# Moving the second norm of half the tokens into the MLP's first half, with five steps of the second matmul summed in DRAM

## The chip, the cores and the metric

The kernel runs on one core of one Trainium2 chip. The metric is the device time of one launch in microseconds. A core has a matrix engine (TensorE, PE in the profile), a vector engine (VectorE, DVE), a scalar engine (ScalarE, ACT), a general engine (GpSimd, POOL) and a queue processor (SyncE, SP). SP and POOL also issue the transfers, on a queue each, in program order. Operands live in SBUF, 128 partitions wide; TensorE writes to PSUM, eight banks of 128 x 512 fp32, and VectorE or ScalarE have to carry the results out. DRAM is the memory beyond.

## What is computed

An adaLN block on 2048 tokens of width 1024: a norm with a scale and a shift from a condition, a Fourier mixing over tokens and width, a gated residual, a second norm with scale and shift, an MLP with 3584 hidden columns, and a second gated residual.

```python
mod = (silu(c) @ w_mod).reshape(1, 6, 1, 1024)
sa, ca, ga, sb, cb, gb = (mod[:, n] for n in range(6))
h = layernorm(x) * (1 + ca) + sa
a, b = h @ dft_hid_re.T, h @ dft_hid_im.T
x = x + ga * (dft_seq_re @ a - dft_seq_im @ b)
h = layernorm(x) * (1 + cb) + sb
x = x + gb * (gelu(h @ w1 + b1) @ w2 + b2)
```

All inputs and the output are fp32.

## The kernel before

Every large product runs in fp16 with each fp32 operand split into a high and a low half, three passes a product. The split takes a copy on ScalarE (the high half) and a subtraction on VectorE (the low half).

**The head** is the part up to the MLP: the first norm, the Fourier transform along the width with its symmetries folded, then the transform along the tokens (`seq_pair`, L3057) in eight blocks b of 256 tokens. For each block `seq_pair` issues two groups of matmuls, Q and P, and two evictions (L3102, L3107). `ln2` (L3171) multiplies by ga (L3213), adds x with an accumulating transfer into SBUF ("xa"), stores the residual stream to the output ("x1", L3225 on SP and L2171 on POOL), and runs the second norm: squares on ScalarE (L3187), subtraction and scale (L3235), a root with one Newton step on 128 x 2 numbers (L2630 to L2639), scale and shift (L3239), squares again, a root again, and a last pass on ScalarE (L3248). `z_psum` (L3347) transposes the block on TensorE (L3368), forms the differences that a seven-product scheme needs with more matmuls (L3376), and splits them from PSUM into fp16 (L3389 on ScalarE, L3416 on VectorE). Block 7 takes `turn` (L3251) and `z_tasks` (L3271), which form the differences on VectorE. The operands of blocks 0 to 3, the first token half, stay in SBUF at `O_ZC`. Those of blocks 4 to 7 go to DRAM (`zc_d`, "fzc" in the profile) on POOL's queue, and `reload` brings them back at chunk 13.

**The MLP** has 28 chunks g of 256 hidden columns: 0 to 13 for the first token half, 14 to 27 for the second. `gemm3(g)` (matmuls at L3843) makes the 256 hidden columns for 1024 tokens with seven products of 12 matmuls, in the order 0, 1, 2, 4, 3, 6, 5. Products share three PSUM banks "a", "g" and "b", from which ScalarE (L3865, gelu at L3862) and VectorE (L3869) evict. Chunks 0 and 1 are made by `gemm3_first` (gelu at L4156). `gemm4(v)` (L3957) multiplies two chunks by their rows of w2, with 14 products in two blocks `blk`. After each product the running sum `acc` (32 KB a partition, at `O_ACC` = 48) is updated: at v = 0 and 7, the first step of each half, four of seven products are copied on ScalarE (L3997) and three added on VectorE (L4007); at all others VectorE does all seven. The chunks run as 0, 1, 2, v = 0, then 3, 4, v = 1, and so on.

During v = 0 to 6, VectorE and ScalarE also split the weights from fp32 to fp16 (L2398, L2410, L2424), after a norm of each piece that sets its scale (L3497, a reduction on POOL at L3509), and SP stores the fp16 pieces (`w1_d`, `w2_d`, "fw"). The second half loads them from there. `w1c` holds two chunks, 14 slots. The bias rows gb x b2 are added to the output by 16 accumulating transfers (`gbb_rows`, L4203, issue at L4208) during chunks 3 to 8.

**The order of the work** is written by a planner in the file that runs when the kernel is built. A task has an engine, a cost, dependencies and a due time; `pick` takes, of the tasks that could start, those due first, and `need` and `emitted` force what a step depends on. Costs are estimates: a root counts 0.4 us on ScalarE, a product `PE12` = 12 x 0.2165 us. Engines then run their lists in order and wait on semaphores.

In the head the planner works on a clock in which the MLP's tasks have due times behind the blocks':

```python
due = 110.0 + 22.0 * b if b < NB - 1 else 300.0
f = lambda: act.activation(dst, src, AF.Gelu_apprx_tanh, scale=inv, bias=b1s[:, 2 * p + j : 2 * p + j + 1])
add("gelu", "act", 0.8, f, [*deps, ("root", NB - 1)], ("quad", g, n), 266.0)
```

The last line makes every gelu wait for the last root of the last block.

Of the kernel before, what the change touches and what calls it, by code (L numbers as in the profile page):

```python
# [9 lines left out]
F32 = mybir.dt.float32  # L10
# [1981 lines left out]
def fast(ctx, tc, x, cre, cim, dre, dim, w1, b1, w2, b2, c, wm, out):  # L1992
# [69 lines left out]
    YW, ZT0 = [((8832, 10880), (12928, 14976), (0, 2048))[b % 3] for b in range(8)], 17024  # L2062
    YW[5] = (53248, 2048)
# [6 lines left out]
    def junk2(key):  # L2070
        return at({("s1", 0): 149.375, ("s1", 1): 46104 / 256, ("s1", 2): 46104 / 256}.get(key, 28.375), 1024, F16).rearrange("p (s x) -> p s x", s=2)
# [32 lines left out]
    def zt(n):  # L2104
        return FA(ZT0 + 1024 * n, (1, 1024))

# [10 lines left out]
    w1c = at(0, 14336, F16).rearrange("p (m s a x) -> p m s a x", m=7, s=2, a=2)  # L2117
# [13 lines left out]
    def raw2(v, q):  # L2131
        return at(O_K + 4 * q, 1024).rearrange("p (s x) -> p s x", s=2)
# [7 lines left out]
    row_d = {n: dram.tile([P, D], F32, tag=f"frow_{n}", name=f"frow_{n}") for n in ("gbb", "gb")}  # L2140
# [61 lines left out]
    class Task:  # L2202
# [16 lines left out]
        def run(self):  # L2219
# [8 lines left out]
            if not in_order[0] and self.eng in ("dma", "st"):  # L2228

                b = self.cost if self.eng == "dma" else 0.8  # L2230
# [38 lines left out]

    def pick_first(until):  # L2270

        first, best = {}, {}
        for q in sorted((q for q in streams.values() if q), key=lambda q: q[0].due):
            t = q[0]
            st = t.start()
            if st > until or st > 1e11:
                continue
# [12 lines left out]
    def pick(until):  # L2290
# [6 lines left out]
        for q in sorted((q for q in streams.values() if q), key=lambda q: q[0].due):  # L2297
# [6 lines left out]
            if t.eng == "dma":  # L2304
# [4 lines left out]
                continue  # L2309
            if best is not None and best[2] or st + t.cost > until:  # L2310
                continue
# [13 lines left out]
    def fill_to(until):  # L2325
        while True:
# [3 lines left out]
            q.popleft().run()  # L2330

# [53 lines left out]
    def split_tasks(q, outs, scale, n, src, res, after, post, last_use, free=None):  # L2385
# [9 lines left out]
        def hi(m, j):  # L2395
# [4 lines left out]
            was = [last_use(k) for k in tup(m)] if last_use is not None else []  # L2400
            t = Task("act", 0.17 + 0.87 * n * len(tup(m)) / 1024, f, reads(j) + was + [free(m) if free else None])
# [483 lines left out]
    def row(n, j):  # L2885
# [57 lines left out]
        add("rowa", "act", 1.1, last_, [k, "mod"], ("rowe", n), due)  # L2943
        if n == 3:
# [112 lines left out]
    def seq_pair(b):  # L3057
# [54 lines left out]
        if b == 5:  # L3112
            deps += [("P", 3), ("Q", 3)]
# [40 lines left out]
    ADDED = (0, 7)  # L3154
# [16 lines left out]
    def ln2(b):  # L3171
        y, w, cl = yb(b), wb(b), lns[b % 3]
# [28 lines left out]
        wfree = w_free(b)  # L3201
        h, k_ = divmod(b, 4)
        yr = FA(YW[b][0] + 1024, (-1, 1024))
        for n in (1, 0):
# [16 lines left out]
            x1[n] = k  # L3221
            if n:
# [5 lines left out]
        else:  # L3228
            step("dve", 0.17, lambda: dve.scalar_tensor_tensor(
                nm, su, -1.0 / D, cm[:, h, k_], op0=ALU.mult, op1=ALU.subtract), ["cm"])  # L3230
# [20 lines left out]
    def turn(i):  # L3251
        b, n = divmod(i, 2)
        ps = PA(6 * 512, (1, 1024))
        due = 100.0 + 11.0 * i

        def f():
            for d in range(ND):
                pe.transpose(ps[:, d * P : (d + 1) * P], wb(b)[:, n, d * P : (d + 1) * P], ident[:, :])

        add("seqt", "pe", 1.5, f, [("w", i), *([("zt", i - 1)] if n else zlast[6] + zlast[7])], ("turn", i), due)  # L3260

        def ev():
            if n and b > 3:
                v = zt(n).rearrange("p (d t) -> p d t", t=P)
                act.activation(v, PA(6 * 512 + P - 1, (P, ND), (-1, P)), AF.Copy)
            else:
                act.activation(zt(n), ps, AF.Copy)

        add("zte", "act", 1.1, ev, [("turn", i)], ("zt", i), due)

    def z_tasks(b):  # L3271
        h, k = divmod(b, 4)
        made = []
        stage = 512 * 184 + 256 if b < NB - 1 else 512 * O_K

        def q(i, j=None):

            o = [ZT0 + 1024 * (n % 2) + 512 * (n // 2) for n in (i, i if j is None else j)]
            return FA(o[0], (o[1] - o[0], 2), (1, 512)) if j is not None else FA(o[0], (1, 512))

        def places(ms, a):
            if h == 0:
                o = [512 * O_ZC[m] + 2048 * a + 512 * k for m in ms]
            else:
                o = [stage + 1024 * made.index(m) + 512 * a for m in ms]
            return HA(o[0], (o[1] - o[0], 2), (1, 512)) if len(ms) > 1 else HA(o[0], (1, 512))

        def hi(ms, js, deps):
            def f():
                if h:  # L3290
                    for m in ms:
                        if 4 < b < NB - 1:
                            reuse("z", (b - 1, len(made)))
                        made.append(m)
                act.activation(places(ms, 0), q(*js), AF.Copy)

            n0 = order.index(ms[0])
            free = [slot("z", (b - 1, n0 + i)) for i in range(len(ms))] if 4 < b < NB - 1 else []
            add("z", "act", 0.17 + 0.44 * len(ms), f, deps + free, (b, "zhi", ms), due, f"z{b}")
            return (b, "zhi", ms)  # L3300

        def lo(ms, js, deps):
            def f():
                dve.tensor_tensor(places(ms, 1), q(*js), places(ms, 0), op=ALU.subtract)  # L3304
                for m in ms:
                    if h:
                        n = made.index(m)
                        dst = zc_d[m][:, :, k].rearrange("p a c t -> p a (c t)")
                        v = HA(stage + 1024 * n, (512, 2), (1, 512))
                        store("z", (b, n), lambda dst=dst, v=v: gp.dma_start(dst, v), ("z", b, m), tag=f"z{b}")  # L3310
                    done["z", b, m] = done[t]

            t = add("z", "dve", 0.13 + 0.54 * len(ms), f, deps, (b, "zlo", ms), due, f"z{b}")
            return t

        def comb(d, a, c, deps, key):
# [991 lines left out]
```

## Time and profile before

| what | value |
|---|---|
| median of 3 runs | 1344.61 us |
| lowest and highest | 1339.23 and 1344.76 us |
| the profiled execution | 1344.03 us |
| its span | 1342.2 us |
| mean granted TensorE clock | 0.962 |
| busy share PE, DVE, ACT, POOL | 92%, 79%, 54%, 19% |
| moved by transfers | 285.23 MB, 213 GB/s |

The profile is one execution. Its busy share of PE counts pipelined matmuls, so a full row of nines says that TensorE always had a matmul under way. The slices and the stretches of time tell where it had not. Waits are given with the engine and line that released them. A line of the code can stand for many shapes and stages: L4007 is one line for all steps of the second matmul, and L2398, L2410 and L2424 are helpers that every split of weights and hidden values goes through.

### The profile page before, as it was taken

Reading aid. Unit: us, or ns where it says so; the run is one execution under the profiler, and the core shown is the slowest. Engines: PE = TensorE matmul, PEld = TensorE weight load, DVE = VectorE, ACT = ScalarE, POOL = GpSimd, SP = SyncE. Lnnn points to the kernel's source line nnn. Section 1 sums busy time; section 2 is a strip of 40 time slices with the busy share of each in tenths; the row PEclk is TensorE's granted clock in tenths of the full one; section 3 lists DMA queues with packets and bytes.
Section 4 is the critical chain, followed back from the end, with each engine's and each line's share of the span. In section 5 each row is a group of like instructions: output and inputs, shape, how many; then the busy total and the mean of one; then the engine's idle time right before and its main releaser. Section 6 shows DMA issues by size and latency. Waiting matters only on the chain.

```text
span 1342.2 us, 16824 instructions
## 1 busy us (share of the span) xinstructions
PE 1230.5 (92%) x5923; PEld 579.8 (43%) x5923; DVE 1060.8 (79%) x1601; ACT 731.1 (54%) x1186; POOL 249.8 (19%) x381
## 2 busy tenths in 40 slices
PE   3568886868999999999999999999999999999997
PEld 0225444544444444444444444444444444444443
DVE  5798777885888898989899896566777868586785
ACT  4785546777767566574746351466455553526330
POOL 2000022332011101010000001435243242233101
PEclk9779787879999999999999999999999999999999
DMA  9966366887269767583625386968595766585155
GB/s 364 389 214 218 117 228 173 188 280 269 97 221 263 227 196 224 162 238 114 220 93 191 118 336 174 287 221 302 199 325 182 234 230 196 190 295 177 56 177 116
DMA packets 103686, 285.23 MB, mean 213 GB/s; under 512 B 13116, under 2 KB 13132, under 8 KB 101672
## 3 DMA queue, kind: packets, MB, share of 16 engines
q1 hardware_dynamic: 75160, 191.44, 41.0%
q0 software_dynamic: 28432, 92.63, 24.2%
q8 instruction: 48, 0.79, 0.2%
q14 instruction: 46, 0.38, 0.1%
HBM read 199.08 MB, written 84.93 MB: 212 GB/s over the span
## 4 chain that ended last, share of the span: by engine, by line
PE 66%; DVE 4%; ACT 2%; DMA 2%; issue 1%; POOL 0%; SPq 0%; DVEq 0%; ACTq 0%; POOLq 0%
PE ps L3957 34%; PE ps L3843 32%; DVE arena L2410 2%; DMA arena<-in_w_dram 1%; ACT arena L2398 1%; DVE arena L2424 1%; DVE arena L4007 1%; DMA fzc<-arena 1%; DVE arena L3869 0%; ACT ps L3497 0%; ACT arena L3862 0%; DVE arena L4059 0%; DVE arena L3304 0%; ACT arena L4156 0%; ACT arena L3997 0%
## 5 line engine op out<-in xcount | busy, mean ns | idle before, releaser
L3843 PE MATMUL ps<-arena 128*128 128x512 f16 x2352 | 513.6, 380 | 5.5 <-ACT arena L3865 3.5
L3957 PE MATMUL ps<-arena 128*128 128x512 f16 x2352 | 510.9, 379 | 2.7 <-DVE arena L4007 1.6
L3843 PEld LDWEIGHTS <-arena 128*128 128x128 f16 x2352 | 230.4, 98 | 285.2 <-issue 7.6
L3957 PEld LDWEIGHTS <-arena 128*128 128x128 f16 x2352 | 230.0, 98 | 281.3 <-issue 3.7
L4007 DVE SCALAR_TENSOR_TENSOR arena<-ps,i4c,arena 128x1024 f32<-128x1024 f32 x179 | 229.3, 1281 | 94.2 <-PE ps L3957 90.0
L2398 ACT ACTIVATE arena<-arena,shc 128x512 f16<-128x512 f32 (+1 forms) x115 | 116.2, 1017 | 129.9 <-DVE arena L2424 74.4
L3727 ACT ACTIVATE arena<-arena 128x512 f32<-128x512 f32 (+4 forms) x159 | 97.2, 613 | 108.6 <-DVE arena L3736 84.5
L2410 DVE SCALAR_TENSOR_TENSOR arena<-arena,shc 128x512 f16<-128x512 f32 (+1 forms) x115 | 128.8, 1121 | 32.4 <-ACT arena L2398 31.9
L2424 DVE TENSOR_TENSOR arena<-arena 128x512 f32<-128x512 f32 (+1 forms) x196 | 148.8, 764 | 4.0
L3862 ACT ACTIVATE arena<-arena,b1s,i1c 128x512 f32<-128x512 f32 x78 | 63.4, 813 | 89.7 <-DVE arena L3869 86.8
L2398 ACT ACTIVATE arena<-arena,s1c 128x512 f16<-128x512 f32 (+1 forms) x70 | 60.7, 886 | 75.6 <-DVE arena L2424 46.3
L3736 DVE TENSOR_TENSOR arena<-arena 128x256 f32<-128x256 f32 x240 | 87.8, 420 | 1.2 <-DMA arena<-in_cre_dram,idxs 0.7
L3869 DVE TENSOR_TENSOR arena<-arena,ps 128x512 f32<-128x512 f32 x78 | 53.4, 685 | 44.1 <-PE ps L3843 42.6
L3509 POOL PARTITION_ALL_REDUCE sums<-sums x21 | 9.2, 444 | 422.7 <-DVE sums L3505 410.3
L2410 DVE SCALAR_TENSOR_TENSOR arena<-arena,s1c 128x512 f16<-128x512 f32 (+1 forms) x70 | 65.8, 958 | 7.2 <-ACT arena L2398 6.9
L3865 ACT ACTIVATE arena<-ps 128x512 f32<-128x512 f32 x78 | 46.0, 589 | 36.1 <-PE ps L3843 36.0
L2410 DVE SCALAR_TENSOR_TENSOR arena<-arena,s2c 128x1024 f16<-128x1024 f32 x49 | 61.9, 1279 | 4.4 <-ACT arena L2398 4.4
L3497 ACT ACTIVATE ps<-arena 128x1024 f32<-128x1024 f32 x46 | 46.7, 1014 | 17.8 <-DMA arena<-in_w_dram 12.2
L2398 ACT ACTIVATE arena<-arena,s2c 128x1024 f16<-128x1024 f32 x49 | 55.0, 1137 | 1.5 <-DVE arena L2424 1.5
L3017 PE MATMUL ps<-arena 128*128 128x256 f16 (+5 forms) x297 | 43.9, 296 | 6.5 <-ACT arena L2796 3.2
L3187 ACT ACTIVATE arena<-arena,lns 128x1024 f32<-128x1024 f32 x32 | 36.6, 1144 | 21.9 <-DMA arena<-in_x_dram,idxm 5.7
L3773 POOL DMA_DIRECT2D arena<-in_cim_dram x69 | 38.1, 558 | 53.1 <-ACT arena L3727 29.0
(239 smaller groups left out, 1123.7 us busy)
## 6 DMA issues: line engine op xcount, KB each, us to landing
fw<-arena SPq DMA_DIRECT2D x71, 512.0 KB
arena<-fw SPq DMA_DIRECT2D x119, 256.0 KB
arena<-fw SPq DMA_DIRECT2D x49, 512.0 KB
arena<-in_wm_dram SPq DMA_DIRECT2D x32, 512.0 KB
arena<-in_w_dram SPq DMA_DIRECT2D x32, 512.0 KB
arena<-in_cre_dram POOLq DMA_DIRECT2D x64, 256.0 KB
arena<-in_cim_dram POOLq DMA_DIRECT2D x64, 256.0 KB
arena<-in_w_dram SPq DMA_DIRECT2D x56, 256.0 KB
```

The costliest lines, as they stand in the source:

```text
L2398: act.activation(o[m][0], q(j), AF.Copy, **sc)
L2410: dve.scalar_tensor_tensor(o[m][1], q(j), scale, o[m][0], op0=ALU.mult, op1=ALU.subtract)
L2424: dve.tensor_tensor(q(d), q(a), q(b), op=op)
L3497: act.activation(junk, parts[j][0], AF.Square, accum_out=t[:, j : j + 1])
L3727: f = lambda: act.activation(v, v, AF.Square, accum_out=csum[0:pn, n : n + 1])
L3736: return lambda: dve.tensor_tensor(dst[0][:, o::2], src[0][:, o::2], dst[0][:, o::2], op=op)
L3843: pe.matmul(ps.rearrange("p (k t) -> p k t", k=4), w1c[:, m, s, a, d * P : (d + 1) * P], zc(m)[:, b, :, d, :], start=(start and d == 0 and ...
L3862: act.activation(dst, src, AF.Gelu_apprx_tanh, scale=inv, bias=b1s[:, 2 * p + j : 2 * p + j + 1])
L3865: after_pe("act", 0.5, lambda: act.activation(quad(g)[:, n], ps[b], AF.Copy), kp[b])
L3869: after_pe("dve", 0.6, lambda: dve.tensor_tensor(q, q, ps[b], op=ALU.add), kp[b])
L3957: pe.matmul(t[:, j], hidc[:, c_, m, a, k * P : (k + 1) * P], w2c[:, m, c_, w], start=(start and c_ == 0 and n == 0), stop=(c_ == 1 and n = ...
L4007: lambda: dve.scalar_tensor_tensor(dst, ps[b], inv, dst, op0=ALU.mult, op1=ALU.add), kp[b],
```

## The change

Blocks 4 to 7 are called HELD. In the head they keep only `seq_pair`, the product with ga, the residual and its store, and the mean. Everything from the squares to the fp16 operands moves to a new function, `z_held`, which works in place on one block at a time, as one chain of steps: blocks 4 and 5 (EARLY_LN = 2) from the copy in SBUF, planned around the MLP's first chunks; blocks 6 and 7 from a copy that is stored to DRAM (`x1_d`) and loaded again, due 100 and 200 us after chunk 2. The rows cb and sb are stored to DRAM; sb is loaded again for every held block, cb for 6 and 7.

```diff
+    HELD = (4, 5, 6, 7)
+    EARLY_LN, W1N = 2, 10
+    def w1_slot(g, m):
+        return (7 * g + ORDER.index(m)) % W1N
...
+            if b in HELD[EARLY_LN:]:
+                store("x1s", i, lambda n=n: sp.dma_start(x1_d[b][:, n], y[:, n]), k)
...
+        if held_:
+            return
...
-        if b < NB - 1:
+        if b not in HELD:
             z_psum(b)
-        else:
-            for n in range(2):
-                turn(2 * b + n)
-            z_tasks(b)
```

`z_held` holds the same passes as `ln2`, with two groups of eight transposes and the differences on VectorE:

```diff
+    def z_held(b, v):
...
+        for n in range(2):
+            step("act", 1.35, sq(n, 1.0, nm), [ld[n], ("nm", b), *(turned(1) if early else [])])
...
+        for n in range(2):
+            step("dve", 1.28, under(n), [k_cb, *([("st", "x1", 2 * b + n)] if early else [])], ("u", b, n))
+        soon.clear()
+        k_sb = load_row("sb", [("st", "crow", 2), *([("P", 7), ("Q", 7)] if v else [])] if early else [])
+        root(0.25 / D, eps4)
...
+        root(0.25 / (SZ * SZ * D**3), epsz)
...
+        for n in range(2):
+            step("pe", 1.1, turn(n), [] if n or not early else zlast[6] if not v else [("held_t", HELD[0])])
+            step("act", 1.1, ev(n), [], ("held_t", b) if n else None)
...
+        hi((0, 1), (0, 2))
+        lo((0, 1), (0, 2))
+        comb((0, 1), (1, 1), (0, 3))
...
+    def due_at(v):
+        return due[3, 2] + 100.0 * (v - 1) if v >= EARLY_LN else 262.0 + 8 * v
```

The gelus of chunks 0 and 1 wait for the last root of block 3 in place of block 7. Chunk 0 uses PSUM banks 3 to 5 in place of 0 to 2. The second block of `gemm4(0)` needs block 4 to be finished, since its running sum lies where block 4 is worked on.

In the second matmul, steps v = 0 to 4 each start `acc` anew (four of seven products copied on ScalarE, three added on VectorE), and their result goes to DRAM; from v = 1 on the transfer adds to what is there. Before v = 5 the sum is loaded back.

```diff
+    def dump(v, blk, m, r, hf, src):
+        dst = acc_d[:, blk, :, r, 512 * hf : 512 * hf + 512]
+        op = {"accum_op": ALU.add} if v else {}
+        store("dump", (v, blk, m), lambda: gp.dma_start(dst, src, **op), ("acc", blk, m), tag=f"dump{v}")
+        if v == NDUMP - 1:
+            f = lambda: sp.dma_start(src, dst)
+            push("back", "back", [Task("dma", 1.5, f, [("st", "dump", (v, blk, m))], ("back", blk, r, hf))], due[4, v + 1] - 30.0)
...
-        first, end = u == 0, v == NPAIR - 1
+        first, end = u == 0 or v < NDUMP, v == NPAIR - 1
...
+        if 0 < v <= NDUMP:
+            need(f"dump{v - 1}", "back")
```

The fp16 pieces of w1 stand in a ring of 10 slots in place of 14, which frees 8 KB a partition. The first piece of w2 is loaded once, earlier and to another place, in place of twice; the next piece's loads no longer wait for block 7. A product calls `turns()`, which puts transposes that are ready ahead of it. The bias rows move from chunks 3 to 8 to chunks 12 and 13:

```diff
     def gbb_rows():
         need("n2_0")
-        t = at(28, 1024)
+        need(*(f"z{b}" for b in HELD))
+        t = at(20, 1024)
...
-            g, m = divmod(i * 42 // NS, 7)
-            push("gbb", "gbb", [Task("pool", 1.5, f, [("g3", 3 + g, ORDER[m])])], 1e6)
+            g, m = divmod(i * 14 // NS, 7)
+            push("gbb", "gbb", [Task("pool", 1.5, f, [("g3", 12 + g, ORDER[m])])], 1e6)
...
-            if g == 2:
+            if g == 11:
                 gbb_rows()
```

More of the change, by code (lines that the diff above doesn't have):

```diff
@@ L4200, in fast @@
     later[0] = True
+    for v, b in enumerate(HELD):
+        if v >= EARLY_LN:
+            z_held(b, v)
     load_w1(3, 0, 1)
```

332 lines of the change are left out of this document (190 added, 142 removed).

## The prediction

> **What bounds the kernel now.** I read the page's slices first, then TensorE in order of time, then its waits, then busy time by stage.
>
> ```profile
> span 1342.2 us, 16824 instructions
> ...
> PE   3568886868999999999999999999999999999997
> ...
> DVE  5798777885888898989899896566777868586785
> ACT  4785546777767566574746351466455553526330
> PEclk9779787879999999999999999999999999999999
> ```
>
> One slice is 33.6 us. PE is full from the tenth slice to the end, and has holes before it, where DVE is busy and the granted clock is lower. So there are two regimes, and the border is what the change can move. TensorE around it, in order of time (columns: start, duration, what, count, idle time before it):
>
> ```profile
> 262.07 2.66 PE L3368 MATMUL ps<-ident,arena 128*128 128x128 f32 x20 [0.58 <-ACT arena L3248]
> ...
> 283.52 2.75 PE L3843 MATMUL ps<-arena 128*128 128x512 f16 x12
> ...
> 304.10 4.45 PE L3843 MATMUL ps<-arena 128*128 128x512 f16 x12 [2.01 <-DMA arena<-fw]
> ...
> 334.91 31.24 PE L3843 MATMUL ps<-arena 128*128 128x512 f16 x144
> 365.99 5.34 PE L3957 MATMUL ps<-arena 128*128 128x512 f16 x24
> ```
>
> L3843 is the first MLP matmul; its first product (12 matmuls) comes at 283.5. By 334.9 only 9 of 21 are done, because the pieces of second norms 4 to 7 lie between them. From there it runs without a break: 144 matmuls, 12 products, take 31.1 us to 365.99, so **2.59 us a product**. At 365.99 the second matmul (L3957) begins, and the remaining 976.2 us of the span (1342.2 - 366.0) are almost pure matmul, as the waits say, before 345 us in the first two rows and after it in the others:
>
> ```profile
> PE ps L3368 <- ACT arena L3248: 17.4, 4, 8.4
> PE ps L3376 <- DVE arena L3416: 8.1, 5, 3.3
> ...
> PE ps L3843 <- ACT arena L3865: 3.5, 3, 2.0
> PE ps L3957 <- DVE arena L4007: 1.6, 3, 1.2
> PE ps L3957 <- ACT arena L3997: 0.8, 2, 0.4
> ```
>
> The head waits for the norm's last pass (L3248) and the fp16 split (L3416), which run on ScalarE and VectorE. By stage (columns of each engine: busy us; then clock, DMA share, GB/s):
>
> ```profile
> 200.00:260.00 60.00, 42.02 (x227) 29.19 (x226) 48.39 (x92) 39.71 (x66) 16.46 (x13) 0.80 0.74 190
> 260.00:335.00 75.00, 57.97 (x294) 32.60 (x292) 56.76 (x111) 58.78 (x92) 23.12 (x28) 0.88 0.82 261
> ...
> 366.00:439.00 73.00, 68.78 (x316) 30.73 (x315) 62.84 (x98) 52.80 (x69) 11.85 (x17) 1.00 0.79 241
> 439.00:511.00 72.00, 71.85 (x334) 32.55 (x333) 67.04 (x94) 43.11 (x57) 5.57 (x8) 1.00 0.72 205
> 511.00:584.00 73.00, 73.00 (x340) 33.04 (x338) 66.89 (x96) 43.62 (x58) 5.55 (x8) 1.00 0.68 199
> 584.00:657.00 73.00, 73.00 (x340) 33.09 (x338) 65.65 (x93) 41.75 (x55) 1.15 (x3) 1.00 0.49 172
> ```
>
> PE idles 35 us between 200 and 335; with three blocks' transposes (2.66 us a block by the row at 262) and their correction matmuls this bounds what can be won at about 45 us. The last four rows are the steps v = 0 to 3: there VectorE is about 90% busy, ScalarE only 57 to 72%.
>
> **Part 1: norms 4 to 7 leave the head.** The MLP's first half needs blocks 0 to 3 only. Its third product needs block 3's last split; VectorE in that stretch:
>
> ```profile
> 264.32 2.48 DVE L3235 SCALAR_TENSOR_TENSOR arena<-arena,lns 128x1024 f32<-128x1024 f32 x2 [0.34 <-ACT arena L3187]
> ...
> 268.70 1.28 DVE L3239 SCALAR_TENSOR_TENSOR arena<-arena,lns 128x1024 f32<-128x1024 f32 x1
> ...
> 273.85 0.16 DVE L2637 TENSOR_TENSOR lns<-lns 128x2 f32<-128x2 f32 x1
> ...
> 280.44 1.23 DVE L3416 TENSOR_TENSOR arena<-ps,arena 128x1024 f16<-128x1024 f32 x1 [1.06 <-ACT arena L3389]
> ```
>
> Pairs of L3235 and L3239 come once a block, so these are block 4's: 2.48 + 2 x 1.28 + nine small ones of 0.16 = 6.5 us that leave the queue ahead of block 3's last split, which ended at 281.7. So it ends at about 275. The y evictions of blocks 4 to 7 stay (bound: if all of those of 5 and 6 slip behind it, 268). Two products are possible before it; the other 19 take 49.2 us: second matmul at 324. On the way lie transfers. SyncE's queue is in order, and today stands behind stores that wait for x to land:
>
> ```profile
> SPq L3225 <- DMA arena<-in_x_dram: 58.6, 6, 21.0
> ```
>
> The w1 loads of the first chunks stand in that queue, now with the second copies of blocks 6 and 7 and two row loads, without the second load of w2. Bounds: 0 and one such wait of 21 us; I take 4, since the stream's own worst wait so far was 2.0. **Second matmul at 328 instead of 366.** If blocks 4 and 5 are not hidden beside these 21 products, this fails first.
>
> **Part 2: what the MLP's first half takes on.** Rows by shape:
>
> ```profile
> L3187 ACT ACTIVATE arena<-arena,lns 128x1024 f32<-128x1024 f32 x30 | 34.3, 1144 | 16.2 <-DMA arena<-in_x_dram,idxm 5.7 <-issue 5.3 <-DMA arena<-in_x_dram 3.0
> L3187 ACT ACTIVATION_READ_ACCUMULATOR arena<-arena,lns 128x1 f32 x30 | 5.7, 188 | 0.0
> L3248 ACT ACTIVATE arena<-arena,lns 128x1024 f32<-128x1024 f32 x16 | 19.1, 1234 | 6.9 <-DVE lns L3246 6.9
> L3258 PE MATMUL ps<-ident,arena 128*128 128x128 f32 x16 | 2.1, 276 | 0.4 <-ACT arena L3267 0.4
> L4156 ACT ACT_TABLE_LOAD x1 | 1.3, 1283 | 0.0
> ...
> L3997 ACT ACTIVATE arena<-ps,i4c x16: 1093/1114/1116, 370.6 to 915.6; 128x1024 f32<-128x1024 f32 x16
> ...
> L4007 DVE SCALAR_TENSOR_TENSOR arena<-ps,i4c,arena 128x1024 f32<-128x1024 f32 x179 | 229.3, 1281 | 94.2 <-PE ps L3957 90.0
> ```
>
> PE: two times 8 transposes a block, 2.1 us; block 4's lie beside the head, three blocks cost **6.3 us**.
> VectorE: 8 evictions a step go over to ScalarE for v = 1 to 4, 32 x 1.28 = 41 us off. A held block adds 2.5 + 2.6 + 1.4 as above, the splits 3 x 1.23 + 0.7 and some 2.6 of differences: 13.5; three add 40.5. Even, still over 90%.
> ScalarE: 8 x 1.11 = 8.9 us more a step; a block adds four squares with their reads (5.3), two passes of L3248 (2.4), and about 7 of copies and roots: 14.6.
>
> **The rule that speaks against it.** In this trace the only table load of the MLP stands before the first gelu, because all roots are done by then. After the change the eight roots of four blocks fall among gelus: up to 16 loads of 1.28 = 20.5 us. With four a block (5.1) ScalarE does 181.3 (the four steps) + 3 x 8.9 + 3 x 19.7 = 267 of 291 us, 92%. The Trainium skill, "ScalarE: Activation LUTs", section "Table sets: the hidden batching unit", says to batch calls by set; its "What ACT_TABLE_LOAD costs" gives 1283 ns, which the row has, and a drain of about 1380 ns more, which no run here shows (the gelu follows at once); 16 such switches would be an estimated 42.6 us.
>
> How much of it reaches PE: two products on one bank pair have another between them, 2.59 us, so an eviction of 1.11 can be 1.5 late; one table load fits, two do not. Bounds: 0, and all 20.5. I take **6 us** for the pressure on both engines, half a microsecond for each of the 12 late loads; the four steps had some 4 until now.
>
> ```profile
> L4208 POOL DMA_DIRECT2D out_dram<-arena x16: 854/1158/1577, 409.5 to 573.7; - x16
> ```
>
> Sums in DRAM: 40 stores of 512 KB on POOL's queue, each read back or added to a step later, about 36 us of first matmuls away; nothing on PE waits nearer. They replace 16 accumulates of bias rows there, and v = 3 has a DMA share of 0.49. I cost them at nothing; uncovered, one landing of some 5 us a step.
>
> Ring of w1 slots, 14 to 10: a slot is refilled 9 products ahead, 23 us; nothing, while VectorE keeps up.
>
> Those 16 bias rows now meet the reload of the second half's operands:
>
> ```profile
> 775.00:780.00 5.00, 5.00 (x25) 2.25 (x23) 4.89 (x6) 1.41 (x2) 0.00 (x0) 1.00 0.98 398
> ...
> 795.00:800.00 5.00, 5.00 (x25) 2.27 (x24) 4.47 (x6) 3.84 (x5) 0.00 (x0) 1.00 1.04 403
> ...
> 773.15 8.09 SPq L3437 DMA_DIRECT2D arena<-fzc  x4
> ```
>
> The DMA engines are full there, at 400 GB/s, and half of the rows (4 MB) would take 10 us of it, between 0 and 10 on PE: I take **4**, since the next chunk needs the operands one by one over 18 us.
>
> **Sum:** 328 + 976.2 + 6.3 + 6 + 4 = 1320.5 of span; around it lay 1.8 (1344.03 - 1342.2): **1322 us**. The median shown is 0.6 above that execution, which I leave out. Its own range is 1301 (268 for block 3, no stalls) to 1336.
>
> **Rivals.**
> A. The head becomes bound by transfers: DMA share is 0.82 already, and one 21 us wait sits before the w1 loads. Second matmul at 345: 1339. Against: 7 MB leave the head (21 stores of 256 KB to fzc, four loads of 512 KB), 4 enter.
> B. Slower: **ScalarE becomes the bound** in v = 1 to 4, its evictions late at every product. From 0.25 us a product over 112 products (28 us) on, the gain is gone; at 0.5 us it is 56 instead of 6: 1372. For: 92% on both engines, bound to each other in order. Against: 16 evictions on ScalarE (L3997) made PE wait 0.8 in all, with ScalarE at 72%.
> C. Table switches, each in front of an eviction: 20.5 in place of 6: 1337. By the Trainium skill's drain as well (page and section above) it would be an estimated 1359.
> D. It doesn't do what it says: blocks 4 and 5 stay ahead of the second matmul on VectorE, 2 x 13.5 us of the 38 gained, and splits of w2 wait behind them: 1322 + 27 = 1349, no change.
>
> **Chances.** Forecast 0.60, A 0.10, B 0.15, C 0.08, D 0.07. A measurement of this kernel can tell about 0.5% (6.7 us) from no change: faster ends at 1337.9. Forecast, half of A and half of C are faster: 0.69; the rest of A and C and D the same: 0.16; B slower: 0.15. The range runs from 1301 to 1349, so that D is within and B, with a few hundredths below, is left out.
>
> **What would show it.** Second matmul (the line of L3957) first at 322 to 335; block 3's last split at 270 to 278; no L3248 of blocks 4 to 7 ahead of the first product. Table loads: up to 16, after the first gelu. PE's waits for ScalarE after 345 us under 15 in all; if far more, B or C. A wait for fzc near the reload of 2 to 8. Wrong it is if PE starts early and then pays it back in holes in v = 0 to 4.

## The result and the profile after

The kernel became slower: 1473.38 us median of 4 runs (1468.47 to 1476.79) against 1343.09 us for the kernel before on the same chip. The ratio is 1.0972 with a 95% interval of 1.0929 to 1.1015, so 130 us were lost where 22 were forecast to be won. No rival of the prediction had a time near this; the slowest, B, had 1372. Two versions further down had one run each far longer than its others (2775.13 and 2154.89 us), and their medians are of the other three. The profiled execution took 1468.47 us. First its page: the span, then the slices of PE, DVE and ACT and the granted clock (a line of three dots stands for rows left out).

```profile
span 1466.7 us, 16907 instructions
...
PE   3567976948989669886989687899999999999996
...
DVE  5788778826777476784947586556676777677784
ACT  4875557628867557673756233236644454536330
...
PEclk9788887979999879998998988999999999999999
```

One slice is 36.7 us. PE has holes up to the 26th slice, some 950 us, where before it was full from the tenth on; behind that it is full as it was. In four of its deepest slices from there (the 9th, 14th, 19th and 23rd) VectorE is at 2, 4, 4 and 5 tenths and ScalarE at 2, 5, 3 and 2. There the engines wait, they do not work. TensorE in order of time, at the head's end:

```profile
274.74 2.75 PE L3915 MATMUL ps<-arena 128*128 128x512 f16 x12
277.82 23.47 PE L3915 MATMUL ps<-arena 128*128 128x512 f16 x108 [0.32 <-DVE arena L3498]
311.74 8.15 PE L3915 MATMUL ps<-arena 128*128 128x512 f16 x24 [10.45 <-DMA arena<-fw]
329.20 10.54 PE L3915 MATMUL ps<-arena 128*128 128x512 f16 x36 [9.31 <-ACT arena L4245]
...
362.35 1.89 PE L4042 MATMUL ps<-arena 128*128 128x512 f16 x8
```

L3915 is the first MLP matmul (L3843 before), L4042 the second (L3957 before). The head starts as forecast: the second product waits 0.32 us for block 3's split (L3498) and starts at 277.82, and ten products are done by 301.3. Then come 10.45 us for weights and 9.31 for an eviction, and the second matmul begins at **362.35**, not at 328. SP's queue, VectorE's next instruction and ScalarE's tell why (start, duration, and in brackets idle time and what ended it):

```profile
285.06 17.09 SPq L3262 DMA_DIRECT2D out_dram<-arena  x2
...
306.04 3.51 SPq L3746 DMA_DIRECT2D arena<-fw  x4
...
317.14 0.47 SPq L3330 DMA_DIRECT2D arena<-frow_sb  x1
```

```profile
324.85 1.28 DVE L3354 SCALAR_TENSOR_TENSOR arena<-arena,csum 128x1024 f32<-128x1024 f32 x1 [25.36 <-DMA arena<-frow_sb]
```

```profile
327.43 1.15 ACT L3318 ACTIVATE arena<-arena,csum 128x1024 f16<-128x1024 f32 x1 [25.51 <-DVE arena L3354]
...
328.58 0.57 ACT L4245 ACTIVATE arena<-ps 128x512 f32<-128x512 f32 x1
```

SP stands for 17 us at the residual stores of the held blocks (L3262), which wait for x to land. Behind them in its one queue are the weights of the first chunks (L3746) and the load of the row sb for block 4 (L3330), issued only at 317.14. VectorE's next instruction (L3354, block 4's scale and shift) waits 25.36 us for that row, ScalarE's squares of the block (L3318) wait 25.51 us for VectorE, and behind them in ScalarE's list stands the eviction (L4245) that TensorE waited 9.31 us for.

Then the steps v = 0 to 3, in the stretches of before (busy us of PE, PEld, DVE, ACT, POOL, then clock, DMA share, GB/s; the sum of all four in the last row):

```profile
...
511.00:584.00 73.00, 57.24 (x243) 24.72 (x243) 50.55 (x70) 45.77 (x61) 12.78 (x17) 0.85 0.69 209
...
sum 291.00, PE 243.06 PEld 109.14 DVE 209.46 ACT 200.42 POOL 53.62; mean PE 60.76 PEld 27.28 DVE 52.37 ACT 50.10 POOL 13.40
```

PE is busy 243 of 291 us. VectorE sank from 90% to 72% (209.5 of 291), ScalarE is at 69% (200.4 of 291), though ScalarE was given more to do in a step and VectorE, by the prediction's sum, as much as before. The granted clock falls to 0.85 in the stretch with most holes, and a matmul takes 0.236 us there on the average (57.24 us for 243) where it took 0.215 before (73.00 for 340). PE's waits from 345 to 950 us (us in total, times, longest):

```profile
PE ps L3915 <- ACT arena L3937: 33.5, 7, 21.6
PE ps L4042 <- ACT arena L4081: 29.3, 7, 12.1
PE ps L4042 <- DVE arena L4092: 25.2, 3, 16.3
PE ps L3915 <- DMA arena<-fzc: 9.7, 3, 3.9
```

All but the last are evictions, but an eviction as such takes about a microsecond, so a wait of 21.6 us is the end of a longer chain. One such chain, from PE back through ScalarE and VectorE to POOL:

```profile
523.34 6.86 PE L3915 MATMUL ps<-arena 128*128 128x512 f16 x18 [21.55 <-ACT arena L3937]
```

```profile
520.96 0.81 ACT L3934 ACTIVATE arena<-arena,b1s,i1c 128x512 f32<-128x512 f32 x1 [22.93 <-DVE arena L3941]
```

```profile
518.28 0.15 DVE L3591 TENSOR_SCALAR sums<-sums 128x1 f32<-128x1 f32 x1 [23.16 <-POOL sums L3587]
```

```profile
498.03 1.21 POOL L4002 DMA_DIRECT2D facc<-arena  x1 [7.19 <-issue]
504.80 1.21 POOL L4002 DMA_DIRECT2D facc<-arena  x1 [5.57 <-issue]
510.92 1.21 POOL L4002 DMA_DIRECT2D facc<-arena  x1 [4.90 <-issue]
...
517.15 0.73 POOL L3417 DMA_DIRECT2D fzc<-arena  x1 [4.26 <-issue]
517.77 0.47 POOL L3587 PARTITION_ALL_REDUCE sums<-sums  x1
```

L4002 is the store of the sums. An accumulating one takes 1.22 us on POOL, but the next mostly starts only 6 to 8 us after the one before (9.6 at most in a row of them), in 11 cases with nothing in the profile that it waits for ("issue"). VectorE is idle from 495 to 518, so it isn't VectorE's work that holds the stores up. Behind three of them and two stores to fzc stands the reduction of a weight piece's norm (L3587, L3509 before), 0.47 us long. VectorE (L3591) needs its result to scale the next split, and stands from 495 to 518. Behind that stands VectorE's eviction L3941; ScalarE's gelu (L3934) waits 22.93 us for it, and the eviction L3937 that TensorE needs stands behind the gelu. VectorE's wait for that reduction, 345 to 950 us in the kernel after and from 366 in the kernel before:

```profile
DVE sums L3591 <- POOL sums L3587: 88.1, 12, 23.2
```

```profile
DVE sums L3513 <- POOL sums L3509: 5.3, 9, 0.6
```

### The profile page after: what moved, and what is told of

It is laid out like the page before. It is cut to its first block, busy times and chain, and to the rows that moved or that the text cites. A ratio compares the mean times of both kernels' runs of the same rounds, so it can differ in the third digit from the quotient of the medians.

```text
span 1466.7 us, 16907 instructions
## 1 busy us (share of the span) xinstructions
PE 1250.3 (85%) x5881; PEld 579.8 (40%) x5881; DVE 1029.4 (70%) x1576; ACT 784.6 (53%) x1236; POOL 300.6 (20%) x430
## 3 DMA queue, kind: packets, MB, share of 16 engines
q0 software_dynamic: 39584, 118.32, 31.1%
## 4 chain that ended last, share of the span: by engine, by line
PE 55%; DVE 14%; issue 11%; DMA 10%; ACT 7%; POOL 2%; SPq 0%; DVEq 0%; POOLq 0%; ACTq 0%
PE ps L4042 26%; PE ps L3915 25%; DVE arena L2433 3%; ACT arena L2420 2%; DMA arena<-in_wm_dram 2%; DMA arena<-fzc 2%; DMA arena<-in_x_dram 2%; DVE arena L2447 1%; DMA arena<-in_x_dram,idxm 1%; PE ps L3043 1%; DVE arena L4092 1%; POOL facc L4002 1%; DMA arena<-in_w_dram 1%; DVE arena L3498 1%; DVE arena L3278 1%
## 5 line engine op out<-in xcount | busy, mean ns | idle before, releaser
L3915 PE MATMUL ps<-arena 128*128 128x512 f16 x2352 | 528.4, 387 | 66.2 <-ACT arena L3937 33.5
L4042 PE MATMUL ps<-arena 128*128 128x512 f16 x2352 | 526.4, 386 | 57.0 <-ACT arena L4081 29.3
L3915 PEld LDWEIGHTS <-arena 128*128 128x128 f16 x2352 | 233.4, 99 | 357.5 <-issue 77.6
L4042 PEld LDWEIGHTS <-arena 128*128 128x128 f16 x2352 | 233.1, 99 | 346.6 <-issue 74.3
L4092 DVE SCALAR_TENSOR_TENSOR arena<-ps,i4c,arena 128x1024 f32<-128x1024 f32 x147 | 188.4, 1282 | 97.0 <-PE ps L4042 94.8
L3934 ACT ACTIVATE arena<-arena,b1s,i1c 128x512 f32<-128x512 f32 x78 | 63.5, 814 | 122.5 <-DVE arena L3941 122.3
L4002 POOL DMA_DIRECT2D facc<-arena x40 | 44.9, 1124 | 230.4 <-DVE arena L4092 87.5
L3941 DVE TENSOR_TENSOR arena<-arena,ps 128x512 f32<-128x512 f32 x78 | 53.3, 684 | 54.2 <-PE ps L3915 52.2
L3937 ACT ACTIVATE arena<-ps 128x512 f32<-128x512 f32 x78 | 46.0, 589 | 43.6 <-PE ps L3915 42.5
L4081 ACT ACTIVATE arena<-ps,i4c 128x1024 f32<-128x1024 f32 x48 | 52.8, 1104 | 28.0 <-PE ps L4042 25.6
L3591 DVE TENSOR_SCALAR sums<-sums 128x1 f32<-128x1 f32 x21 | 3.2, 151 | 92.0 <-POOL sums L3587 92.0
L3043 PE MATMUL ps<-arena 128*128 128x256 f16 (+5 forms) x297 | 47.1, 309 | 9.3 <-DVE arena L2575 3.4
```

The lines of the kernel that those rows point to most:

```text
L3043: pe.matmul(PA(bp + o, (1, w), pn=m), l, r, start=i == 0, stop=i == len(mm_) - 1)
L3915: pe.matmul(ps.rearrange("p (k t) -> p k t", k=4), w1at(g, m)[:, a, d * P : (d + 1) * P], zc(m)[:, b, :, d, :], start=(start and d == 0 an ...
L3941: after_pe("dve", 0.6, lambda: dve.tensor_tensor(q, q, ps[b], op=ALU.add), kp[b])
L4002: store("dump", (v, blk, m), lambda: gp.dma_start(dst, src, **op), ("acc", blk, m), tag=f"dump{v}")
L4042: pe.matmul(t[:, j], hidc[:, c_, m, a, k * P : (k + 1) * P], w2c[:, m, c_, w], start=(start and c_ == 0 and n == 0), stop=(c_ == 1 and n = ...
L4092: lambda: dve.scalar_tensor_tensor(dst, ps[b], inv, dst, op0=ALU.mult, op1=ALU.add), kp[b],
```

## The experiments

Each was timed against the kernel before on the same chip. Ratios are to that kernel, with 95% intervals; differences between versions are of medians.

**The sums in eight DRAM tensors instead of one.** It asks whether the stores wait for each other because they write to one tensor.

```diff
-    acc_d = dram.tile([P, 2, 2, 2, D], F32, tag="facc", name="facc")
+    acc_d = {k: dram.tile([P, 2, 512], F32, tag=f"facc_{k}", name=f"facc_{k}") for k in range(8)}
...
-        dst = acc_d[:, blk, :, r, 512 * hf : 512 * hf + 512]
+        dst = acc_d[4 * blk + 2 * r + hf][:, :, :]
```

> The changed kernel, but the running sums in DRAM are eight tensors (one for each quadrant of each block) in place of one; plan, queues and bytes are the same. Theory P (POOL's queue): each of the 40 stores to the one tensor waits until the store before it has landed, 6 to 8 us apart, and the norm's sums over partitions stand behind them in POOL's queue. Then VectorE's wait for those sums falls from 88 us to under 25, and the time from 1473 to 1385 to 1415 us. Rival B (ScalarE and VectorE overloaded, the one of the prediction): within 1% of 1473. Rival Q (the transfers as such are too many): within 1% of 1473.

Measured: 1470.97 us, 1.0956 (1.0915 to 1.0998), the same as with one tensor. That the stores form a chain by their tensor (theory P) is refuted. Rivals B and Q both had this time.

**No sums in DRAM.** `acc` stays in SBUF and is added to at every step, all else as in the change.

```diff
-    NDUMP = 5
+    NDUMP = 0
...
```

> The changed kernel without the sums in DRAM: the running sum stays in SBUF as before, VectorE adds at all steps but v = 0 and 7; norms 4 to 7 stay within the MLP's first half. Theory P: as e1_tiles, 1380 to 1415 us, since no store stands in POOL's queue. Rival B: VectorE gets 41 us back, so no faster than the changed kernel, 1470 to 1500. Rival Q: 20 MB of accumulating transfers less, about 1400.

Measured: 1396.46 us, 1.0405 (1.0368 to 1.0443): 77 us of the 130 go with the stores, though VectorE has the 41 us of additions back that they saved it. Rival B, by which this would not be faster, fails here; P's range and Q's (about 1400) both hold the result. The second matmul still came first at 363.46. VectorE's wait for the reduction is as good as gone:

```profile
DVE sums L3591 <- POOL sums L3587: 8.8, 8, 3.0
```

**The stores alone, in the kernel before.** 32 extra stores of the running sum in v = 1 to 4, of the same shape and on POOL, from v = 2 on accumulating; nothing reads them. Once into one tensor, once into eight.

```diff
...
+    def dump(v, blk, m, r, hf, src):
+        dst = acc_d[:, blk, :, r, 512 * hf : 512 * hf + 512]
+        op = {"accum_op": ALU.add} if v > 1 else {}
+        store("dump", (v, blk, m), lambda: gp.dma_start(dst, src, **op), ("acc", blk, m), tag=f"dump{v}")
...
+                if 0 < v < 5 and m in (1, 3, 6, 5):
+                    dump(v, blk, m, r, hf, dst)
```

> The kernel before, with 32 extra stores of the running sum to one DRAM tensor after the products of v = 1 to 4 (accumulating from v = 2 on), which nothing reads; no engine but POOL has more to do. Theory P: 30 to 80 us slower than before, with VectorE waiting for POOL's sums 25 us or more in place of 5. Rival B: within 0.5% of before. Rival Q: 30 us or more slower, and e4 the same.

> As e3, the extra stores to eight tensors. Theory P: within 1% of before. Rival B: within 0.5% of before. Rival Q: as slow as e3.

Measured: 1369.28 us, 1.0207 (1.0167 to 1.0247), and 1369.52, 1.0208 (1.0167 to 1.0249). The stores cost 26 us with none of the change's other parts. That is a little under the 30 that P and Q had, and the number of tensors again makes no difference, as only Q had it. So up to here the stores are shown as a cost and POOL's queue as the way, but not what it is about them. VectorE's wait for the reduction from 345 to 950 us, with one tensor, was 29.5 us in 9 cases.

**The same bytes in half as many pieces.** A store took half of a row for two tokens of a partition, 256 pieces of 2 KB; now it takes whole rows, 128 pieces of 4 KB. Number of stores and bytes stay; the four of a block start in two pairs, when a whole row is ready.

```diff
-        dst = acc_d[:, blk, :, r, 512 * hf : 512 * hf + 512]
+        if m not in (6, 5):
+            return
...
+        for j in range(2):
+            a, d = acc[:, blk, j, r], acc_d[:, blk, j, r]
+            store("dump", (v, blk, r, j), lambda a=a, d=d: gp.dma_start(d, a, **op), ("acc", blk, m), ("acc", blk, 3 if r else 1), tag=f"dump{v}")
...
```

> The changed kernel with the running sums stored as whole rows (128 pieces of 4 KB a transfer) in place of quadrants (256 pieces of 2 KB); bytes and number of transfers are the same, those of a block go out in two pairs. Theory R (what POOL waits for is room or time that goes with the number of pieces, as one tensor or eight made no difference in e1): VectorE's wait for POOL's sums falls from 88 us to about 45, and the time from 1473 to 1415 to 1440 us. Rival S (an accumulating 512 KB takes its 5 to 6 us whatever its pieces): within 1% of 1473.

Measured: 1401.13 us, 1.0428 (1.0392 to 1.0464), which is 72 us less and within 5 us of having no sums in DRAM. POOL in order of time, and VectorE's wait:

```profile
487.27 1.82 POOL L4005 DMA_DIRECT2D facc<-arena  x2 [13.55 <-DVE arena L4095]
488.42 1.25 POOL L3587 PARTITION_ALL_REDUCE sums<-sums  x1
489.79 0.89 POOL L4005 DMA_DIRECT2D facc<-arena  x1
493.21 0.85 POOL L4005 DMA_DIRECT2D facc<-arena  x1 [2.52 <-issue]
...
639.15 2.76 POOL L4005 DMA_DIRECT2D facc<-arena  x3 [4.05 <-DVE sums L2192]
...
648.09 0.86 POOL L4005 DMA_DIRECT2D facc<-arena  x1 [6.18 <-issue]
```

```profile
DVE sums L3591 <- POOL sums L3587: 28.5, 9, 10.3
```

A store (L4005 here) takes 0.9 us in place of 1.22, and three, where they are ready, fall into 3.4 us or less where the others took 6 to 8 each; the fourth then waits 1 to 6 us. The gain is larger than theory R had it (1415 to 1440 us), and Q, which counts transfers and bytes alone, fails. So nearly the whole price of the sums in this kernel lay in the shape of their transfers. The later start of two of the four stores is in this number too and was not tried apart.

**The row sb from POOL's queue**, in the version with whole rows and in the one with no sums in DRAM.

```diff
-            return step("dma", 1.5, lambda: (sp if early else gp).dma_start(row_, row_d[name][:, :]), deps, ("hr", b, name))
+            return step("dma", 1.5, lambda: gp.dma_start(row_, row_d[name][:, :]), deps, ("hr", b, name))
...
```

> As e5, and the rows sb for blocks 4 and 5 are loaded from POOL's queue, which is idle then, in place of SyncE's, where they stand behind the residual's stores. Theory H (the head lost its gain because VectorE stood 25 us at block 4's step that needs this row): the second matmul begins at 335 to 345 in place of 362, and the time is 15 to 25 us below e5. Rival: the head is bound elsewhere (w1 loads in the same queue), second matmul at 355 or later, within 7 us of e5.

> e2 (no sums in DRAM) with the sb rows from POOL's queue. Theory H: second matmul at 335 to 345 in place of 363, 1370 to 1382 us in place of 1396. Rival: within 7 us of 1396.

Measured: 1383.47 us, 1.0289 (1.0257 to 1.0321), and 1385.55, 1.0322 (1.0284 to 1.036): 18 and 11 us less. The second matmul came first at 349.1 and 348.0 in place of 363, later than the 335 to 345 of theory H, and only the first of the two times is within H's range. SP still stands 17.4 us at the residual stores, and now the weights behind them are what TensorE waits for, 10.1 us in the first of the two and 10.6 in the second.

**No switches of ScalarE's tables.** In the version with no sums in DRAM, the square roots of the held blocks are replaced by the identity, so their norms aren't computed; the instruction stays.

```diff
...
-            step("act", 0.4, lambda: roots(ve, r, va, scale, bias))
+            step("act", 0.4, lambda: roots(ve, r, va, scale, bias, AF.Identity))
```

> e2 with the square root of the held blocks' norms replaced by the identity: these blocks' norms are not computed, but the same instructions run, without the 12 table loads (15 us of ScalarE). If table loads reach TensorE (rival C of the prediction): 8 to 20 us below 1396. If they fit beside the products: within 5 us of 1396.

Measured: 1390.98 us, 1.0335 (1.0295 to 1.0376), against 1396.46 with them. The twelve extra loads are worth some 5 us by the medians, between what the two theories had, and the two intervals touch, so the size is uncertain. In the profiled executions the second matmul came first 8 us earlier (355.2 for 363.5) and the rest of the span took 6 us longer, so no gain shows in the MLP itself.

**The first weights from POOL too**, with whole rows and with no sums in DRAM.

```diff
                 need("st_w1s")
-                sp.dma_start(w1at(g, m), w1_d[g][:, m])
+                gp.dma_start(w1at(g, m), w1_d[g][:, m])
```

> The kernel with whole-row sums and the sb row on POOL (1383.47 us), with the loads of the first chunks' weights (line of L3746) issued by POOL instead of SP, so that they no longer stand behind SP's x1 stores; in that kernel TensorE waited 10.14 us for them, and its second matmul came first at 349.08 us. Theory H (the head is held by SP's in-order queue alone): the wait goes, the second matmul comes first at 339 to 341 us, and the time is 8 to 11 us less, 1372 to 1376. Theory V (by then VectorE and ScalarE, which take the held blocks' splits and the evictions in one order, are as late as the weights): the wait moves to an eviction of the first products, the second matmul still comes first at 346 to 349, and the time is within 3 us of 1383.

> No sums in DRAM at all (they stay in SBUF), the sb row and the first chunks' weights loaded by POOL. By theory H the time is 8 to 11 us under the same without the weights' move (1385.55 us), 1375 to 1378; by theory V within 3 us of it. Against the kernel with whole-row sums and both moves it tells what the sums in DRAM still cost: within 5 us of each other, as 1385.55 and 1383.47 were, if whole rows cost nothing on the path.

Measured: 1383.55 us, 1.0314 (1.029 to 1.0339), and 1383.92, 1.0299 (1.027 to 1.0329): within 2 us of the versions without the move. Theory H fails. The second matmul came first at 351.4 and 350.7, nearer to V's 346 to 349 than to H's 339 to 341, but not for V's reason. VectorE in the first of the two, and the stretch of its wait:

```profile
313.94 1.28 DVE L3354 SCALAR_TENSOR_TENSOR arena<-arena,csum 128x1024 f32<-128x1024 f32 x1 [12.03 <-DMA arena<-frow_sb]
```

```profile
304.00:314.00 10.00, 4.89 (x23) 2.13 (x22) 0.06 (x1) 0.34 (x1) 3.33 (x7) 0.95 1.03 407
```

The row sb now stands behind the weights in POOL's queue and lands late again; VectorE and ScalarE do nothing in these 10 us, and the transfers move 407 GB/s at a full DMA share.

**The bias rows over three chunks instead of two**, on top of that.

```diff
-            g, m = divmod(i * 14 // NS, 7)
+            g, m = divmod(i * 21 // NS, 7)
```

> The same with the sixteen adds of the bias rows spread over three chunks of the first matmul instead of two. Theory B (these adds stand in POOL's queue before a norm reduction of the weights and cost the one eviction wait near the reload, 9.3 us in the kernel with whole-row sums and the sb row on POOL): the wait falls under 4 us and the time is 5 to 9 us under the kernel without the spread. Theory N (that wait belongs to the reload of the sums, which is not moved): the two are within 2 us of each other.

Measured: 1382.96 us, 1.0315 (1.0281 to 1.0349), the same. The largest wait for VectorE's eviction fell from 10.7 to 4.5 us, near what theory B had, but waits for fzc rose from 0.7 to 3.8 us and the time stayed, as N had it. It looks as if the collision is spread and not removed; the trace doesn't settle it.

**One held block more in the MLP.** The version with whole rows and both loads on POOL, with only block 4 beside the first products; block 5 goes through DRAM like 6 and 7.

```diff
-    EARLY_LN, W1N = 2, 10
+    EARLY_LN, W1N = 1, 10
```

> The kernel with whole-row sums and the sb row and first weights on POOL (1383.55 us), with only block 4's second norm beside the first products; block 5's takes the way of blocks 6 and 7, through DRAM and late, among the steps of the MLP's first half. In that kernel the second matmul came first at 351.2 us, after one wait of 9.4 us for an eviction on ScalarE at the head's end, and TensorE's waits from 362 to 950 us were 41.7 us. Theory D (the two held blocks stand ahead of the first products' evictions in the lists of ScalarE and VectorE, and that is what is left of the head's delay): the wait at the head goes, the second matmul comes first at 338 to 344 us, and what the block costs later is less than that, so the time is 1372 to 1380. Theory K (a held block costs TensorE about the same wherever it lies, because VectorE and ScalarE stop each other in order): the head gains some 10 us, the waits from 362 to 950 us rise to 50 or more, and the time is within 4 us of 1383.5.

Measured: 1415.39 us, 1.0535 (1.0511 to 1.0559), 32 us more. The head gains 6.6 us (second matmul at 344.8 for 351.4), and the MLP loses 38. PE's waits from 330 to 1000 us, with two blocks beside the head and then with one:

```profile
PE ps L4045 <- ACT arena L4084: 16.2, 7, 5.3
PE ps L3915 <- ACT arena L3937: 11.5, 7, 3.6
PE ps L4045 <- DVE arena L4095: 10.7, 1, 10.7
```

```profile
PE ps L4045 <- ACT arena L4084: 27.9, 6, 7.4
PE ps L3915 <- ACT arena L3937: 18.1, 11, 3.1
PE ps L4045 <- DVE arena L4095: 12.0, 2, 11.8
```

L4084 and L3937 are ScalarE's evictions of the two matmuls. Waits for fzc rose too, from 0.7 to 9.1 us. The late block costs the MLP 38 us where its passes on VectorE were put at 13.5, and both theories fail on the time: D had 1372 to 1380, and K, whose rise of the waits came true, 1383.5 within 4 us.

**The residual stores of the held blocks from POOL**, in the version with whole rows and the sb row on POOL.

```diff
-                store("x1", i, lambda: sp.dma_start(o_s[h, 4 + k_], y[:, 0]), k)
+                store("x1", i, lambda: (gp if held_ else sp).dma_start(o_s[h, 4 + k_], y[:, 0]), k)
```

> The kernel with whole-row sums and the sb row on POOL (1383.47 us), in which SP also no longer issues the residual stores of the held blocks that wait for x to land (line of L3262 for blocks 4 to 7): POOL issues them, behind the loads that they wait for. SP is then free for the first weights from some 285 us on, and the sb row keeps its place in POOL's queue, ahead of no weights. With the sb row on POOL TensorE waited 10.14 us for weights; with the weights on POOL as well it waited 9.41 us behind the sb row instead, and in both the transfers were at 360 to 416 GB/s from 301 us on. Theory O (only the order of issue costs the 10 us): both waits go, the second matmul comes first at 337 to 342 us, and the time is 1370 to 1376. Theory T (from 301 us on the head is bound by the transfers themselves, which is rival A of the prediction; whatever goes first makes another one late): one wait of 5 us or more for a load or behind the sb row stays, the second matmul comes first at 345 us or later, and the time is 1380 to 1388.

Measured: 1381.51 us, 1.0291 (1.025 to 1.0333), 2 us less than without the move and no gain clear of the noise, with the second matmul at 345.4. PE's waits from 262 to 362 us (VectorE stood 10.2 us for the sb row):

```profile
PE ps L3915 <- ACT arena L4244: 5.5, 1, 5.5
PE ps L3915 <- DMA arena<-fw: 5.2, 1, 5.2
```

By its numbers theory T holds. But SP was not free as meant. The line that came next in its queue, the stores of `x1_d` (L3258), waits for x to land as well:

```profile
SPq L3258 <- DMA arena<-in_x_dram: 11.8, 2, 8.2
SPq L3258 <- DMA arena<-in_x_dram,idxm: 8.9, 1, 8.9
```

So the order of issue is not excluded as the cause of these last 10 us, and a version that frees both lines wasn't tried.

No version beat the kernel before; the best stay 3% behind it.

## Why the prediction was wrong

**Block 3's split: right.** Forecast to end at 275, with a band of 270 to 278; it ended at 277.77.

**"Sums in DRAM … I cost them at nothing": the step that failed.** In this kernel they cost 72 us by the shape of their transfers and 77 in all, with VectorE's 41 us of additions set off against them; alone, in the kernel before, 32 of them cost 26, so most of the rest comes from their meeting other parts of the change, which was not taken apart. Even the price given for a lost cover, one landing of some 5 us a step, is 20 to 25 us for the five steps. The step looked at who waits for the stored data, found the next user 36 us away, and stopped there. It did not list what is queued behind a store on POOL: the weight norms' reductions, which have nothing to do with the sums and feed VectorE within a step. The rows to see it stood in the trace of before, where POOL's reduction made VectorE wait 5.3 us in nine cases with little else in the queue. A sign of the hold-up stood there as well: of the bias rows, which accumulate too, three went out in 2.75 us and the fourth only 3.47 us after them, with no wait shown (L4208, from 409.54). What that trace could not show is that an accumulating store of 256 pieces holds up the next one for 6 to 8 us. The sign given for B or C, far more than 15 us of waits for ScalarE, came too (33.5 + 29.3 us), but the chain behind it led on to POOL.

**The head's transfers, 4 us: the second failure.** The second matmul came 38 us behind the 324 that the prediction had without them. The prediction named the queue, the stall (21 us as upper bound) and even the two row loads in it. But it took its 4 us from the wait of the weights' stream so far, and put no price on VectorE's wait for the sb row, behind which the evictions in the lists of VectorE and ScalarE stand. The two moves of that load gave back 18 and 11 us. With it moved, and both blocks still beside the head, the second matmul comes at 345 to 351 in six versions, which is near **rival A's** number (345); the transfers do run at a full share there. Whether they or the order of issue bind is left open.

**The pressure on VectorE and ScalarE, 6 us: too small, for a reason that busy shares don't show.** In the version with whole rows and both loads on POOL, 1028.9 us lie from the second matmul to the end (1380.3 - 351.4) in place of 976.2 (1342.2 - 366.0), 52.7 more. Its windows:

```profile
351.00:650.00 299.00, 271.31 (x1241) 122.98 (x1240) 233.58 (x369) 223.56 (x289) 53.60 (x78) 0.98 0.72 216
650.00:950.00 300.00, 285.84 (x1316) 128.68 (x1315) 217.86 (x294) 151.05 (x214) 62.23 (x77) 0.98 0.87 259
```

PE's waits up to 950 us are 41.7 us against 4.5 before, 37 more; the transposes were put at 6.3; and 2% of 557 us of matmuls at a clock of 0.98, where it was 1.00 before, is an estimated 11. Together that is 54, about the 52.7. VectorE is at 75% there (451 of 599), ScalarE at 63%. What changed is how long VectorE stops, in the split's two halves and at POOL's reduction. In this version, from 351 to 950 us, and in the kernel before, from 366:

```profile
DVE arena L2433 <- ACT arena L2420: 35.7, 35, 3.8
...
DVE sums L3591 <- POOL sums L3587: 28.7, 9, 10.3
```

```profile
DVE arena L2410 <- ACT arena L2398: 14.8, 11, 3.8
```

VectorE has about as much to do for a matmul as it had (451.4 us beside 2557 matmuls here, 489.7 beside 2684 before), but stands 44 us more for the others (35.7 + 28.7 against 14.8 + 5.3). Each list is in order, so an eviction behind such a stop waits with it. **Rival B** had the place and the sign right and the mechanism at most half: ScalarE is not full, at 63%. That the two are bound to each other instead is a reading of these waits and not shown. Against it as the whole account: without sums in DRAM and with both loads on POOL, VectorE's two stops are only 22.7 + 8.7 us while it is busy 81% (486.7 of 599), TensorE's waits there are 40 us and the time is the same. What was tried is the dose: one more late block costs 32 us. That blocks 6 and 7 cost as much each was not measured.

**Table loads: right in size.** Twelve more came, up to 16 were foreseen, and they are worth some 5 us, near the half microsecond each that was taken. The Trainium skill, "ScalarE: Activation LUTs", section "What ACT_TABLE_LOAD costs", would put them at 12 times 2.66 us, an estimated 32; taking them away gave back 5.5 us. The trace has the 1283 ns of the load and shows no time for a drain, here in the version with both loads on POOL, where the load follows on a split that ends at 301.03, and the gelu on the load:

```profile
301.05 1.28 ACT L4244 ACT_TABLE_LOAD   x1
302.34 0.78 ACT L4244 ACTIVATE arena<-ps,b1s,i1c 128x512 f32<-128x512 f32 x1
```

**The reload: 9.7 us for fzc** where 4 were taken, inside the bounds of 0 and 10. In the versions with whole rows it is 0 to 0.7 us, but 3.8 with the bias rows over three chunks and 9.1 with a third block late. **The shorter ring of w1** cost nothing that shows: no wait for weights after the head. **Rival D** was not what happened: blocks 4 and 5 were worked on beside the first products as planned, and it was in the main their row and not their work that came late; with block 5 taken away the head gained 6.6 us.

Of the whole: 130 us lost are 72 of the sums' pieces, 18 of the sb row, and 40 that no version took away, made of a head that gains 15 us in place of 38 and an MLP that pays 53. The first two are shown by taking them away; the cause of the last 40 is argued from traces and stays open.

## What to carry to other kernels

A transfer that nobody waits for is not free: walk the queue that issues it, write down what stands behind it, and who needs that. Count its pieces as well as its bytes, and make a row of SBUF one piece where the layout allows it. And don't take idle time for room: here VectorE was busy 75% and ScalarE 63% with two late blocks, and a third, a chain of steps that crosses between them, still cost 32 us.

## What the runs showed of the hardware

An accumulating store of 512 KB issued by POOL let the next one follow mostly after 6 to 8 us in 256 pieces of 2 KB. In 128 pieces of 4 KB three that were ready went out in 2.7 us and the fourth 1 to 6 us after them, though bytes and count of stores were equal. The kernels are 72 us apart.

The profile's pages count the packets of the queue that POOL fills (the software queue). It had 29728 without sums in DRAM and 39584 with them, 9856 more for 8 plain stores (v = 0) and 32 accumulating ones. The kernel before had 28432 and with the extra stores 36112, 7680 more for 8 plain and 24 accumulating. Both come out with 144 packets for a plain store and 272 for an accumulating one of the same shape. In whole rows it had 35488: 5760 more than without sums, 144 for each of the 40. So whole rows changed the packets of the accumulating stores alone. And the 0.72 to 0.74 us that a plain store took on POOL differ from the 1.22 of an accumulating one not by the adding alone: at 144 packets that takes 0.9 us. Eight DRAM tensors, in which a store finds its 4 KB of a partition in one piece, left the packets at 39584 and the time the same.

The Trainium skill, "DMA: Bandwidth & Descriptors", section "Anatomy of one DMA — SWDGE (gpsimd) path", has descriptor generation as small and says that many can be emitted before its cost shows. Whether the 6 to 8 us seen here go into making the descriptors or into waiting for room to put them is open. That three small stores go out at once and only then one waits speaks for room; a larger room wasn't tried.
